# Retuned due times of a list scheduler, and five output buffers claimed ahead of the delta matmul

## Chip, cores and metric

The kernel runs on one core of one Trainium2 chip. The metric is device time in microseconds (us) of one execution. Runs are called "slow" when they lie over 1.5% above the fastest run of the same kernel. The experiments were made on three chips, with the kernel before run again beside them; its fast runs took 199.5, 199.9 and 201.6 us in the mean of each. A ratio is always to the kernel before.

## The reference, cut

Sliding-window attention, followed by a mixture of low-rank adapters over the attention output.

```python
# q, k, v: (8 batches, 8 heads, 576, 64) float32
scores = q @ k^T / 8;  masked to |i - j| <= 32
attn = softmax(scores);  x = (attn @ v) as rows of 4608 x 512
logits = x @ w_gate                       # 8 experts
w = softmax over the two largest logits   # the gate
delta = sum over the two: w * ((x @ A[e]) @ B[e])   # rank 16
return x + delta
```

## The kernel before

The program records pieces of work (`P.op`: engine, modelled duration, due time, what it depends on). A list scheduler then decides the order in which they are emitted. In the traces TensorE's pieces come in that order. So the due times change no arithmetic, only the order on each engine.

```python
# scheduler, cut: for each engine, of the pieces that can start within 0.12 us
# of the earliest one, take the one with the smallest due time
t0 = min(t for t, _ in c)
t, o = min(((t, o) for t, o in c if t <= t0 + slack),
           key=lambda x: (x[1]["due"], x[1]["i"]))
...
# PSUM buffers in the scheduler's model: strictly in turn
slots, cnt = self.pools[o["alloc"]]
prev = slots[cnt[0] % len(slots)]
```

The pieces of one batch are these (names as in the profile). Every matmul of this kernel writes a tile of the two pools in the memory PSUM; the other tiles lie in the memory SBUF.

- Loads of q, k, v on the SP queue, and casts to 16 bits on GpSimd (`c`, `vbd`).
- For each of 4 head pairs: two groups of six transposes (`tp`, then copies `qT` and `kT`), score blocks (`ps`, then `PT` by exp), and PV (`po`, then reciprocal `rc` and `xb`).
- For each batch: transposes of x (`tx`, copied to `xT`), the gating matmul `pz`, the gate on VectorE with one exp on ScalarE (result `zs`), its transposes `tz` (copied to `zT`), the delta matmuls `pd` (three pieces), output copies `obt`, and stores.

```python
ob_pool = tc.alloc_tile_pool(name="ob", bufs=3)
pw = tc.alloc_tile_pool(name="pw", bufs=3, space=PSUM)   # ps, po, pz, pd
pt = tc.alloc_tile_pool(name="pt", bufs=2, space=PSUM)   # tp, tx, tz
...
# gate on VectorE; lg lies in PSUM (pz), all other operands in SBUF
m1 = max(lg);  is1 = lg >= m1;  lm = is1 * -1e30 + lg;  m2 = max(lm);  dm = m2 - m1
dm = exp(dm)                                        # ScalarE
is2 = lm >= m2;  s = dm + 1;  s = 1 / s;  is2 = is2 * dm
gate = is1 + is2;  gate = gate * s;  zs = pz * gate
...
pd = P.op("PE", 0.43 * len(gs), d, ..., [ez, c_perm], alloc="w")
o  = P.op("ACT", ..., d, ..., [pd] + P_pd.get(len(P_pd) - 3, []))   # waits for a store
s_ = P.op("SP", 0.45 * len(gs), d + 3, ..., [o])                    # the store
```

The softmax here doesn't subtract the row's maximum and nothing guards it: scores larger than these inputs give would overflow.

## Time and profile before

| | before |
|---|---|
| device time, median of the first 3 runs | 199.71 us (199.14 to 202.63) |
| span of the profiled run | 196.4 us |
| TensorE busy | 144.3 us, 73% |
| VectorE, ScalarE, GpSimd busy | 58%, 43%, 43% |
| mean TensorE clock | 0.931 |

These lines are from the page of the kernel before. The digits are 40 slices of 4.9 us each, in tenths (9 is 90% or more). PEclk is the granted TensorE clock.

```profile
span 196.4 us, 4088 instructions
...
PE 144.3 (73%) x1600; PEld 103.8 (53%) x1600; DVE 113.8 (58%) x290; ACT 84.9 (43%) x109; POOL 84.1 (43%) x91
...
PE   0047978968389898698496898995699879958270
...
PEclk9999999999958999999669999999669999999966
DMA  5999999989999999999999589850042005102315
```

No engine is full. The DMA row is near 9 up to slice 26 (about 128 us) and then low, yet TensorE looks no busier after it than before. The clock row has three dips in the middle, at slices 12 to 13, 20 to 21 and 29 to 30, and one at the end.

The next lines are the timeline of all engines around the second dip (start, duration, engine, line, operation, output and inputs; in brackets the idle time before, and what ended it).

```profile
91.83 4.33 POOL L203 CAST vbd<-r 64x2304 f16<-64x2304 f32 x2 [3.81 <-PE po L437]
91.92 2.06 DVE L521 TENSOR_TENSOR gate<-gate,s 128x40 f32<-128x40 f32 x1
...
94.02 0.82 DVE L523 TENSOR_TENSOR zs<-pz,gate 128x640 f16<-128x640 f32 x1
...
94.89 1.01 PE L396 MATMUL ps<-mask,ident 128*128 128x512 f16 x2 [2.30 <-DVE zs L523]
...
98.52 0.61 PE L546 MATMUL pd<-B_sb,zT 128*128 128x512 f16 x1 [1.22 <-ACT zT L538]
```

A GpSimd cast starts at 91.83 us. The VectorE operation that starts just after it has 40 elements per partition and takes 2.06 us. Behind it `zs` comes late, and the score block at 94.89 us had waited 2.30 us for it, because its PSUM buffer was still held by `pz`, which `zs` reads. The delta matmul at 98.52 us waited another 1.22 us, and it starts at half clock.

The TensorE timeline of the kernel before shows another kind of wait.

```profile
79.25 0.38 PE L548 MATMUL pd<-xb,perm 128*128 128x512 f16 x1
81.22 0.92 PE L437 MATMUL po<-vbd,PT 128*128 128x130 f16 x13 [1.59 <-ACT obt L553]
```

A PV matmul waits 1.59 us for the PSUM buffer of an output copy, and that copy waits for an output buffer, which means for a store. In the waits view of the kernel before (total us, times, longest) the kinds add up as follows.

```profile
ACT obt L553 <- DMA out_dram<-obt: 6.1, 2, 3.2
...
PE ps L396 <- DVE zs L523: 4.7, 2, 2.4
...
PE po L437 <- ACT obt L553: 3.3, 2, 1.7
...
PE tp L352 <- DVE qT L358: 0.9, 1, 0.9
```

Last comes the table of stretches of the kernel before. Each stretch reaches from the last delta matmul of one batch to that of the next (columns: length, busy time of PE, PEld, DVE, ACT and POOL, granted clock, DMA share, GB/s).

```profile
60.30:79.03 18.73, 16.81 (x208) 12.61 (x206) 11.46 (x33) 8.95 (x12) 12.09 (x9) 1.00 1.11 292
79.03:102.47 23.44, 18.17 (x197) 12.99 (x196) 13.55 (x34) 11.74 (x15) 9.31 (x7) 0.85 1.06 284
102.47:123.29 20.82, 17.20 (x207) 12.64 (x205) 11.63 (x34) 10.76 (x15) 9.26 (x7) 1.00 0.87 236
123.29:145.61 22.32, 18.34 (x198) 13.11 (x196) 14.15 (x34) 10.37 (x14) 10.29 (x14) 0.85 0.32 98
145.61:164.04 18.43, 16.74 (x208) 12.61 (x206) 11.46 (x33) 10.55 (x14) 0.00 (x0) 1.00 0.14 50
```

A batch takes 18.4 to 23.4 us for 16.7 to 18.3 us of TensorE. The fourth and fifth line have little transfer left and are hardly faster (22.3 and 18.4 us; the second and first took 23.4 and 18.7 us).

### The profile page before, as it was taken

To read this page: it belongs to the slowest core of one execution; us is meant where nothing else is said; L and a number is where in the kernel's file an instruction comes from. 1 tells how busy PE (TensorE), PEld (TensorE's weight loads), DVE (VectorE), ACT (ScalarE), POOL (GpSimd) and SP (SyncE) were. 2 spreads that over 40 slices of the span, in tenths; PEclk is the share of its full clock that TensorE was granted. 3 is DMA by queue.
4 is the path that set the end of the run, shared out by engine and by line. 5 is a ranking of instruction groups with operands and counts; after the bars stand their busy time and mean duration, and the time that the engine had idled before them with its cause. 6 is when DMAs were issued, how large, how long until landed. Compare 5 with 4: busy or idle time off the path is not lost. (4 is left out here: it accounts for less than half of the span.)

```text
span 196.4 us, 4088 instructions
## 1 busy us (share of the span) xinstructions
PE 144.3 (73%) x1600; PEld 103.8 (53%) x1600; DVE 113.8 (58%) x290; ACT 84.9 (43%) x109; POOL 84.1 (43%) x91
## 2 busy tenths in 40 slices
PE   0047978968389898698496898995699879958270
PEld 0024656757237774487345674774358656845220
DVE  6876354846923873477812774759617774675500
ACT  0033354540347434653253636741465367625050
POOL 7976666748659628182507208496000000000000
PEclk9999999999958999999669999999669999999966
DMA  5999999989999999999999589850042005102315
GB/s 151 196 209 233 310 271 231 323 199 267 332 196 284 305 197 337 346 202 270 306 299 254 165 282 243 213 200 0 0 169 75 0 3 188 53 3 106 134 33 209
DMA packets 85810, 38.28 MB, mean 195 GB/s; under 512 B 44192, under 2 KB 81184, under 8 KB 85792
## 3 DMA queue, kind: packets, MB, share of 16 engines
q1 hardware_dynamic: 78464, 36.58, 68.9%
q0 software_dynamic: 4832, 0.27, 4.2%
q10 hardware_dynamic: 2496, 1.18, 2.3%
q8 instruction: 12, 0.20, 0.4%
q14 instruction: 6, 0.05, 0.1%
HBM read 28.85 MB, written 9.44 MB: 195 GB/s over the span
## 5 line engine op out<-in xcount | busy, mean ns | idle before, releaser
L352 PE MATMUL tp<-ident,c 128*128 128x128 f16 (+1 forms) x384 | 35.9, 215 | 22.0 <-POOL c L189 12.4
L408 ACT ACTIVATE PT<-ps 128x1024 f16<-128x1024 f32 x36 | 36.6, 1025 | 33.5 <-PE ps L401 33.4
L203 POOL CAST vbd<-r 64x2304 f16<-64x2304 f32 (+1 forms) x20 | 34.9, 1747 | 23.4 <-DMA out_dram<-obt 9.3
L189 POOL CAST c<-r 128x1024 f16<-128x1024 f32 (+1 forms) x36 | 31.7, 899 | 28.0 <-issue 14.4
L352 PEld LDWEIGHTS <-c 128*128 128x128 f16 (+1 forms) x384 | 25.3, 100 | 34.0 <-POOL c L189 13.1
L437 PE MATMUL po<-vbd,PT 128*128 128x130 f16 x416 | 30.1, 222 | 4.6 <-ACT obt L553 3.3
L358 DVE COPY qT<-tp 128x576 f16<-128x576 f16 x32 | 14.5, 454 | 32.0 <-PE tp L352 32.0
L437 PEld LDWEIGHTS <-PT 128*128 128x128 f16 x416 | 25.3, 98 | 7.1 <-ACT obt L553 3.9
L368 ACT COPY kT<-tp 64x576 f16<-64x576 f16 x32 | 20.3, 634 | 19.1 <-DVE kT L366 17.2
L553 ACT COPY obt<-pd 128x1024 f32<-128x1024 f32 (+1 forms) x24 | 20.4, 872 | 16.0 <-PE pd L548 8.3
L451 DVE TENSOR_TENSOR xb<-po,rc 128x640 f16<-128x640 f32 x32 | 26.4, 825 | 1.1
L396 PE MATMUL ps<-mask,ident 128*128 128x512 f16 x72 | 22.8, 400 | 4.7 <-DVE zs L523 4.7
L401 PEld LDWEIGHTS <-kT 128*128 128x128 f16 x288 | 20.3, 102 | 10.6 <-issue 1.7
L401 PE MATMUL ps<-qT,kT 128*128 128x128 f16 x288 | 24.3, 228 | 0.3 <-ACT kT L368 0.2
L546 PE MATMUL pd<-B_sb,zT 128*128 128x512 f16 x40 | 18.9, 473 | 5.6 <-ACT zT L538 5.6
L548 PE MATMUL pd<-xb,perm 128*128 128x512 f16 x40 | 18.7, 468 | 0.0
L480 DVE COPY xT<-tx 128x512 f16<-128x512 f16 x40 | 15.8, 419 | 4.1 <-PE tx L473 2.9
L366 DVE COPY kT<-tp 64x576 f16<-64x576 f16 x32 | 14.3, 446 | 5.5 <-PE tp L352 5.3
L450 DVE RECIPROCAL rc<-po 128x10 f32<-128x10 f32 x32 | 6.8, 214 | 15.1 <-PE po L437 15.1
L473 PE MATMUL tx<-ident,xb 128*128 128x128 f16 x160 | 14.2, 218 | 1.4 <-DVE xT L480 0.5
L473 PEld LDWEIGHTS <-xb 128*128 128x128 f16 x160 | 10.6, 97 | 2.6 <-issue 1.9
L513 ACT ACTIVATE dm<-dm 128x5 f32<-128x5 f32 x8 | 1.7, 208 | 22.8 <-DVE dm L511 22.8
(44 smaller groups left out, 111.1 us busy)
## 6 DMA issues: line engine op xcount, KB each, us to landing
r<-in_v_dram SPq DMA_DIRECT2D x24, 288.0 KB, 5.9
r<-in_q_dram SPq DMA_DIRECT2D x12, 512.0 KB, 5.7
r<-in_k_dram SPq DMA_DIRECT2D x12, 512.0 KB, 6.2
out_dram<-obt SPq DMA_DIRECT2D x24, 256.0 KB, 3.0
out_dram<-obt SPq DMA_DIRECT2D x16, 192.0 KB, 2.9
r<-in_q_dram SPq DMA_DIRECT2D x22, 128.0 KB, 4.0
r<-in_v_dram SPq DMA_DIRECT2D x16, 144.0 KB, 3.8
r<-in_k_dram SPq DMA_DIRECT2D x14, 128.0 KB, 4.9
```

Of the source, the lines that this page charges most:

```text
L189: eng.tensor_copy(out=qk[b, w][:, g, :, n0:n1].rearrange("p j n e d -> p e n j d"), in_=raw[b, w][:, g, :, n0:n1].rearrange("p e n (j d) - ...
L203: eng.tensor_copy(out=dst[64 * e:64 * e + 64, NB * n0:NB * n1, VD * e:VD * e + D], in_=raw[b, 2][64 * e:64 * e + 64, NB * n0:NB * n1])
L352: nc.tensor.matmul(out=o, lhsT=src[:, g, j, n] if g < 2 else sx[p0:p0 + 32, j, n], rhs=ident[p0:p0 + np_, p0:p0 + np_], is_transpose=True, ...
L368: nc.scalar.copy(out=o, in_=kt[64:128])
L396: nc.tensor.matmul(out=ps[:, i:i + 4], lhsT=ident, rhs=mask.rearrange("p r h j k -> p (r h j k)"), start=True, stop=False)
L401: nc.tensor.matmul(out=ps[:, i], lhsT=kTs[u % NQ][:, a, :], rhs=qTs[u % NQ][:, :, 32 * a:32 * a + 64].rearrange("p j (h k) -> p h j k", h= ...
L408: nc.scalar.activation(out=PTs[t % NPT][:, :, 64:192], in_=holder["t"], func=AF.Exp, scale=1.0 / float(D) ** 0.5)
L437: nc.tensor.matmul(out=po[:, GS * g:GS * g + 2 * VD], lhsT=PTs[t % NPT][:, sl, off:off + 128], rhs=vbd[b % NV][:, n, a, :], start=(i == 0) ...
L451: nc.vector.tensor_tensor(out=xs[b].rearrange("p g (e n d) -> p g e n d", e=2, n=NP)[:, :, :, n], in0=pog[:, :, :, 0:D], in1=bcast(rc, 3, ...
L473: nc.tensor.matmul(out=tp[:, 128 * c:128 * c + 128], lhsT=xs[b][:, g, 128 * c:128 * c + 128], rhs=ident, is_transpose=True, start=True, st ...
L546: nc.tensor.matmul(out=pd[:, i], lhsT=zT[:, g], rhs=B_sb, start=True, stop=False)
L553: nc.scalar.copy(out=ob[:, 0:len(gs)], in_=holder["t"][:, 0:len(gs)])
```

## The change

The change sets all due times anew, so that the scheduler's own model of the program is short. The model also gets longer transfers, five output buffers, and a claim: a delta matmul is not placed before the output buffer is free. The claim exists in the model alone; no wait is added on the hardware. Cut to its core:

```diff
+DUE = dict(ld=-10.42, cqk=-6.15, cv=-3.48, tq=-3.24, tk=-2.87, s=-0.73, e=-19.89,
+           pv=-0.4, nm=1.98, tx=-0.8, txs=0.14, pz=0.7, g0=3.1, g3=1.41, tz=2.88,
+           pd=3.21, pds=0.86, st=-7.0)
+    NOB = 5
-    ob_pool = tc.alloc_tile_pool(name="ob", bufs=3)
+    ob_pool = tc.alloc_tile_pool(name="ob", bufs=NOB)
-                xfer = P.op("DMA", (4.6 if w == 2 else 3.4) * f, d + w / 10,
+                xfer = P.op("DMA", (5.5 if w == 2 else 3.9) * f, d + w / 10,
-        e = P.op("DVE", 1.0, due_u(u, 0), lambda: norm(u, h),
+        e = P.op("DVE", 1.0, due_u(u, DUE["nm"]), lambda: norm(u, h),
-                      [ez, c_perm], alloc="w")
+                      [ez, c_perm] + P_pd.get(len(P_pd) - NOB, []), alloc="w")
-                     lambda ...: moe_ob(b, gs, h), [pd] + P_pd.get(len(P_pd) - 3, []))
+                     lambda ...: moe_ob(b, gs, h), [pd])
-            s_ = P.op("SP", 0.45 * len(gs), d + 3, ...)
+            s_ = P.op("SP", 0.45 * len(gs), d + DUE["st"], ...)
  ... (every other due time replaced in the same way)
```

This is the TensorE order around the gate of batch 2, read from the two built programs:

```
before: pz(2) | T16q T16k po14 po15 T17q T17k  ps18  tz(2) pd(2) pd(2) T18q T18k pd(2) ps19 T19q tx(3) ...
after:  pz(2) | T16q T16k ps16 T17q ps17 T17k po14 po15 T18q tz(2) ps18 T18k pd(2) tx(3) pd(2) tx(3) tx(3) ps19 ...
```

`T16q` is the transpose group of q for head pair 16. After the change more work stands between `pz` and the first piece that needs its buffer, and other work stands between `tz` and `pd` and among the `pd`.

More of the change, by code (lines that the diff above doesn't have):

```diff
@@ L301, in plan_loads @@
             f = (n1 - n0) / 4
-            d = due_u(4 * b, -7 + n0 / 4)
+            d = due_u(4 * b, DUE["ld"] + n0 / 4)
             done = {}
@@ L321, in plan_loads @@
                            + [P_pv.get(4 * (b - NV) + i) for i in range(4)])
-                    c = P.op(ce, 4.3 * f, due_u(4 * b, -2.5 + n0 / 4),
+                    c = P.op(ce, 4.3 * f, due_u(4 * b, DUE["cv"] + n0 / 4),
                              lambda n0=n0, n1=n1: cast_v(b, cn_v, n0, n1), dep)
@@ L329, in plan_loads @@
                     c = P.op(ce, (2.2 if w < 2 else 1.1) * f + (0.2 if f < 1 else 0),
-                             due_u(4 * b, -4 + n0 / 4), fn, dep)
+                             due_u(4 * b, DUE["cqk"] + n0 / 4), fn, dep)
                 for n in range(n0, n1):
@@ L373, in plan_T @@
         h = {}
-        t = P.op("PE", 0.32, due_u(u, -3), lambda: transposes(u, 0, h),
+        t = P.op("PE", 0.32, due_u(u, DUE["tq"]), lambda: transposes(u, 0, h),
                  [P_cast[b, 0, n], P_cast[b, 3, n], c_ident] + war, alloc="t")
-        e = P.op("DVE", 0.40, due_u(u, -3), lambda: evac_q(u, h), [t] + war)
+        e = P.op("DVE", 0.40, due_u(u, DUE["tq"]), lambda: evac_q(u, h), [t] + war)
         use(t, e)
         h2 = {}
-        t2 = P.op("PE", 0.32, due_u(u, -2.9), lambda: transposes(u, 1, h2),
+        t2 = P.op("PE", 0.32, due_u(u, DUE["tk"]), lambda: transposes(u, 1, h2),
                   [P_cast[b, 1, n], P_cast[b, 3, n], c_ident] + war, alloc="t")
-        e0 = P.op("DVE", 0.40, due_u(u, -2.9), lambda: evac_k(u, 0, h2), [t2] + war)
-        e1 = P.op("ACT", 0.60, due_u(u, -2.9), lambda: evac_k(u, 1, h2), [t2, e0] + war)
+        e0 = P.op("DVE", 0.40, due_u(u, DUE["tk"]), lambda: evac_k(u, 0, h2), [t2] + war)
+        e1 = P.op("ACT", 0.60, due_u(u, DUE["tk"]), lambda: evac_k(u, 1, h2), [t2, e0] + war)
         use(t2, e0, e1)
@@ L416, in plan_S @@
         h = {}
-        s = P.op("PE", 0.90, due_u(u, -1.5), lambda: score(t, h),
+        s = P.op("PE", 0.90, due_u(u, DUE["s"]), lambda: score(t, h),
                  [c_ident] + [e for x in t_units(t) for e in P_T[x]]
                  + ([P_pv[x] for x in t_units(t - NPT)] if t >= NPT else []), alloc="w")
-        e = P.op("ACT", 0.97, due_u(u, -1.5), lambda: exp(t, h),
+        e = P.op("ACT", 0.97, due_u(u, DUE["e"]), lambda: exp(t, h),
                  [s, c_PT[t % NPT]] + ([P_pv[x] for x in t_units(t - NPT)]
@@ L457, in plan_pv @@
         h = {}
-        p = P.op("PE", 0.76, due_u(u, 0), lambda: pv(u, h),
+        p = P.op("PE", 0.76, due_u(u, DUE["pv"]), lambda: pv(u, h),
                  [P_exp[t] for t in s_tiles(u)] + [P_cast[b, 2, n]] + P_x.get(b - 3, []),
                  alloc="w")
-        e = P.op("DVE", 1.0, due_u(u, 0), lambda: norm(u, h),
+        e = P.op("DVE", 1.0, due_u(u, DUE["nm"]), lambda: norm(u, h),
                  [p] + [x for x in P_x.get(b - 3, [])])
@@ L566, in plan_moe @@
             h = {}
-            t = P.op("PE", 0.23, due_u(U, 0.1 + g / 10), lambda g=g, h=h: moe_tx(b, g, h),
+            t = P.op("PE", 0.23, due_u(U, DUE["tx"] + g * DUE["txs"]), lambda g=g, h=h: moe_tx(b, g, h),
                      [P_norm[4 * b + n] for n in range(NP)], alloc="t")
-            e = P.op("DVE", 0.37, due_u(U, 0.1 + g / 10), lambda g=g, h=h: moe_xT(b, g, h),
+            e = P.op("DVE", 0.37, due_u(U, DUE["tx"] + g * DUE["txs"]), lambda g=g, h=h: moe_xT(b, g, h),
                      [t] + [P_pz.get(b - 2)])
@@ L572, in plan_moe @@
             ev.append(e)
-        pz = P.op("PE", 1.2, due_u(U, 1.0), lambda: moe_zl(b), ev + [c_w], alloc="w")
+        pz = P.op("PE", 1.2, due_u(U, DUE["pz"]), lambda: moe_zl(b), ev + [c_w], alloc="w")
         P_pz[b] = pz
-        d0 = P.op("DVE", 1.0, due_u(U, 1.1), lambda: moe_gate(b, 0), [pz])
-        d1 = P.op("ACT", 0.2, due_u(U, 1.1), lambda: moe_gate(b, 1), [d0])
-        d2 = P.op("DVE", 0.2, due_u(U, 1.15), lambda: moe_gate(b, 2), [d0])
-        d3 = P.op("DVE", 1.7, due_u(U, 1.4), lambda: moe_gate(b, 3),
+        d0 = P.op("DVE", 1.0, due_u(U, DUE["g0"]), lambda: moe_gate(b, 0), [pz])
+        d1 = P.op("ACT", 0.2, due_u(U, DUE["g0"]), lambda: moe_gate(b, 1), [d0])
+        d2 = P.op("DVE", 0.2, due_u(U, DUE["g0"] + 0.05), lambda: moe_gate(b, 2), [d0])
+        d3 = P.op("DVE", 1.7, due_u(U, DUE["g3"]), lambda: moe_gate(b, 3),
                   [d1, d2] + P_zs.get(b - 2, []))
@@ L581, in plan_moe @@
         h = {}
-        tz = P.op("PE", 0.28, due_u(U, 2.0), lambda: moe_tz(b, h), [d3], alloc="t")
+        tz = P.op("PE", 0.28, due_u(U, DUE["tz"]), lambda: moe_tz(b, h), [d3], alloc="t")
         P_zs[b] = [tz]
-        ez = P.op("ACT", 0.65, due_u(U, 2.0), lambda: moe_zT(b, h),
+        ez = P.op("ACT", 0.65, due_u(U, DUE["tz"]), lambda: moe_zT(b, h),
                   [tz] + P_zT.get(b - 2, []))
@@ L589, in plan_moe @@
             h = {}
-            d = due_u(U, 2.3 + 0.5 * i)
+            d = due_u(U, DUE["pd"] + DUE["pds"] * i)
             pd = P.op("PE", 0.43 * len(gs), d, lambda gs=gs, h=h: moe_pd(b, gs, h),
-                      [ez, c_perm], alloc="w")
+                      [ez, c_perm] + P_pd.get(len(P_pd) - NOB, []), alloc="w")
             o = P.op("ACT", 0.93 if len(gs) == 2 else 0.53, d,
-                     lambda gs=gs, h=h: moe_ob(b, gs, h), [pd] + P_pd.get(len(P_pd) - 3, []))
+                     lambda gs=gs, h=h: moe_ob(b, gs, h), [pd])
             use(pd, o)
-            s_ = P.op("SP", 0.45 * len(gs), d + 3, lambda gs=gs, h=h: moe_st(b, gs, h), [o])
-            x = P.op("DMA", 0.7 * len(gs), d + 3, lambda: None, [s_])
+            s_ = P.op("SP", 0.45 * len(gs), d + DUE["st"], lambda gs=gs, h=h: moe_st(b, gs, h), [o])
+            x = P.op("DMA", 0.7 * len(gs), d + DUE["st"], lambda: None, [s_])
             P_pd[len(P_pd)] = [x]
```

## The prediction

> **What bounds it now.** No engine is full. The page gives TensorE 144.3 us busy of 196.4 (73%), VectorE 58%, ScalarE 43%. The table of stretches shows three regimes. Up to about 58 us the loads set the pace: in the timeline the transposes of batches 1 and 2 wait 1.7 and 2.5 us for GpSimd casts. From 60 to 146 us a batch takes 20.9, 21.3, 21.5 and 22.0 us with 17.4 to 18.0 us of TensorE, although the transfers have mostly stopped by 130 us: the order of work, not the data, is the limit. From the last gating matmul, 172.4 us, 24.0 us of serial tail follow.
>
> The idle TensorE time has three sources (waits and timeline). (1) The gate: a score block waits 2.30 and 2.42 us for zs, because its PSUM buffer is held by pz. The chain is lengthened by VectorE: a 40-element multiply that normally takes 0.20 us took 2.06 us while GpSimd cast v from 91.83 us. This agrees with the Trainium skill, "SBUF — State Buffer", section "Who interferes with whom": a VectorE operation with two SBUF inputs is blocked by a GpSimd operation that reads SBUF. (2) The delta matmul waits 0.4 to 1.2 us for zT. (3) With three output buffers and stores queued behind loads (the first store is issued at 74.2 us), an output copy waits for a store, holds its PSUM buffer, and TensorE idles 1.59 and 1.69 us. Besides, the clock is 0.50 for about 6 us after each gap of kind 1, where a 512-column matmul takes 0.43 instead of 0.22 us; some 3 us are lost each time.
>
> **What changes.** No arithmetic is added or removed. In the instruction order, after the gate matmul two score blocks and four transpose groups (3.6 us from traced issue spacings) come before the first PV matmul that needs pz's buffer; zs is ready about 4.3 us after pz. A score block and a transpose group stand between tz and the delta matmul, delta matmuls alternate with the next batch's transposes, and VectorE does the normalizations after the gate. The stores of batches 0 to 3 stand before later loads, and five buffers remove wait 3. GpSimd's order hardly changes. The claim ahead of the delta matmul only steers the order; no hardware wait is added.
>
> **Cost.** Summed traced spacings give 15.4 us of TensorE per batch; with 7% of unlisted small gaps and 0.7 us of gate wait, 17.2 us (estimate). Batch 3 cannot start before its casts at 57.8 us, so nothing is won until there; loads with stores need about 16.7 us per batch (issue times), slightly under. Batch 7's transposes start at about 57.8 + 4 x 17.2 = 127 us instead of 153; the following stretch is 43 us as before, since the tail keeps its serial gate and its store. Span about 170; device time lies 2 to 3 us higher, plus an occasional slow-clock episode: **174 us**, 80% range 166 to 185. Faster by over 2%: 0.95; within 2%: 0.04; slower: 0.01.
>
> **What would show it.** Batches near 17 us between 60 and 125 us; waits for zs under 1 us each; no output copy waiting for a store; stretches at clock 0.50 fewer in the middle; the last 24 us unchanged; DMA share near 1 up to 115 us, with TensorE perhaps waiting for casts of batches 5 to 7.
>
> **What would make it wrong.** Casts colliding with the gate at new moments (up to 2 us per batch, directly exposed); loads falling behind stores, so that batch 5 to 7 transposes wait; the clock dropping more often since it follows short gaps; an order tuned to a model whose latencies differ.

## The result

The changed kernel takes 175.41 us in the median of 4 runs (173.06 to 177.03); beside it, the kernel before took 201.17 us in the median of 4. The ratio is 0.868 (95% interval 0.858 to 0.879). A ratio is the mean time of one kernel's fast runs over that of the other's of the same rounds, so it is not quite the ratio of the medians. The changed kernel's fast runs took 173.06 and 174.03 us, its slow ones 176.79 and 177.03 us.

These are the same lines of the page after the change (a slice is now 4.3 us).

```profile
span 172.3 us, 4079 instructions
...
PE 137.2 (80%) x1600; PEld 103.4 (60%) x1600; DVE 113.8 (66%) x290; ACT 85.0 (49%) x109; POOL 85.0 (49%) x91
...
PE   0028596699957999999599989997999899969180
...
PEclk9999999659995699999999999999999999999968
DMA  5999999999999899999999997976889603403425
```

TensorE is 80% busy and the clock no longer dips in the middle. A new dip stands at slices 8 and 9 (30 to 39 us), while the first batches wait for data. One is left at slices 13 and 14 (52 to 60 us), and one at the very end.

This is the table of stretches after, again from one batch's last delta matmul to the next one's.

```profile
62.33:78.42 16.09, 15.73 (x202) 12.29 (x201) 12.12 (x33) 11.06 (x15) 10.33 (x8) 1.00 1.07 272
78.42:94.98 16.56, 14.75 (x190) 11.39 (x188) 12.09 (x33) 9.94 (x14) 9.74 (x8) 1.00 1.07 268
94.98:112.07 17.09, 16.61 (x217) 13.00 (x215) 12.56 (x35) 10.87 (x15) 9.10 (x7) 1.00 0.99 283
112.07:128.35 16.28, 14.88 (x192) 11.44 (x189) 11.93 (x33) 10.18 (x14) 7.87 (x12) 1.00 0.78 220
128.35:145.77 17.42, 16.56 (x214) 13.00 (x213) 13.65 (x35) 10.75 (x15) 3.00 (x4) 1.00 0.52 157
```

A batch now takes 16.1 to 17.4 us, and TensorE is busy for 89 to 98% of it. The work of VectorE and ScalarE is the same as before (62.35 against 62.26 us and 52.80 against 52.36 us over the five stretches). TensorE's busy time fell from 87.27 to 78.54 us although it does the same matmuls: part of that is the clock, which was 0.85 in two of the stretches of before. The place of the gain can be read off the starts of these last delta matmuls: batch 0 at 60.30 us before and 62.33 after (2.0 us lost), batch 5 at 164.04 and 145.77 (20.3 us won in between), end at 196.4 and 172.3 (5.8 us won in the rest).

In the waits view after, the wait of score blocks for `zs` and the waits of PV and output copies for a store are gone. One wait has grown from 0.9 us to 8.1 us.

```profile
PE tp L360 <- DVE qT L366: 8.1, 9, 1.8
...
PE po L445 <- DVE zs L531: 0.4, 1, 0.4
```

The largest of these nine, in the timeline after:

```profile
82.94 1.04 POOL L197 CAST c<-r 128x1024 f16<-128x1024 f32 x1 [0.88 <-DMA r<-in_q_dram]
...
83.21 0.79 DVE L519 TENSOR_TENSOR dm<-m,m 128x5 f32<-128x5 f32 x1
83.92 0.44 DVE L366 COPY qT<-tp 128x576 f16<-128x576 f16 x1
...
84.41 0.38 PE L360 MATMUL tp<-ident,c 128*128 128x128 f16 x4 [1.81 <-DVE qT L366]
```

The 5-element subtraction `dm` normally takes 0.17 us. Here it takes 0.79 us beside a GpSimd cast, and `qT` stands behind it in VectorE's queue. So the cast still holds up the gate; but TensorE now loses 1.81 us once here, not 2.30 and 1.22 us and then the clock.

### The profile page after: what moved, and what is told of

Its sections match the earlier page's. It is cut to its first block, busy times and chain, and to the rows that moved or that the text cites. A ratio compares the mean times of both kernels' runs of the same rounds, so it can differ in the third digit from the quotient of the medians.

```text
span 172.3 us, 4079 instructions
## 1 busy us (share of the span) xinstructions
PE 137.2 (80%) x1600; PEld 103.4 (60%) x1600; DVE 113.8 (66%) x290; ACT 85.0 (49%) x109; POOL 85.0 (49%) x91
## 4 chain that ended last, share of the span: by engine, by line
PE 63%; DMA 13%; DVE 11%; ACT 4%; SPq 2%; issue 2%; ACTq 2%; POOL 1%
PE po L445 13%; PE tp L360 10%; DMA r<-in_k_dram 10%; PE ps L404 8%; PE ps L409 7%; PE pz L497 6%; PE pd L554 6%; PE tx L481 5%; PE pd L556 5%; DMA r<-in_q_dram 3%; DVE dm L519 2%; SPq L175 2%; ACT PT L416 2%; PE tz L541 2%; DVE qT L366 2%
## 5 line engine op out<-in xcount | busy, mean ns | idle before, releaser
L360 PE MATMUL tp<-ident,c 128*128 128x128 f16 (+1 forms) x384 | 37.0, 219 | 23.8 <-POOL c L197 11.6
L360 PEld LDWEIGHTS <-c 128*128 128x128 f16 (+1 forms) x384 | 26.3, 101 | 34.5 <-POOL c L197 12.8
L197 POOL CAST c<-r 128x1024 f16<-128x1024 f32 (+1 forms) x36 | 32.3, 906 | 28.2 <-DMA r<-in_k_dram 15.3
L376 ACT COPY kT<-tp 64x576 f16<-64x576 f16 x32 | 20.3, 634 | 32.1 <-DVE kT L374 31.7
L445 PE MATMUL po<-vbd,PT 128*128 128x130 f16 x416 | 28.7, 220 | 1.1 <-ACT PT L416 0.7
L409 PEld LDWEIGHTS <-kT 128*128 128x128 f16 x288 | 21.7, 107 | 10.6 <-issue 3.6
L404 PE MATMUL ps<-mask,ident 128*128 128x512 f16 x72 | 24.5, 426 | 0.0
L554 PE MATMUL pd<-B_sb,zT 128*128 128x512 f16 x40 | 16.0, 400 | 1.6 <-ACT zT L546 1.6
L556 PE MATMUL pd<-xb,perm 128*128 128x512 f16 x40 | 15.9, 399 | 0.0
L481 PE MATMUL tx<-ident,xb 128*128 128x128 f16 x160 | 13.3, 221 | 0.0
L497 PE MATMUL pz<-WA_sb,xT 128*128 128x136 f16 x160 | 10.8, 223 | 0.0
```

The source lines that it names most:

```text
L197: eng.tensor_copy(out=qk[b, w][:, g, :, n0:n1].rearrange("p j n e d -> p e n j d"), in_=raw[b, w][:, g, :, n0:n1].rearrange("p e n (j d) - ...
L360: nc.tensor.matmul(out=o, lhsT=src[:, g, j, n] if g < 2 else sx[p0:p0 + 32, j, n], rhs=ident[p0:p0 + np_, p0:p0 + np_], is_transpose=True, ...
L404: nc.tensor.matmul(out=ps[:, i:i + 4], lhsT=ident, rhs=mask.rearrange("p r h j k -> p (r h j k)"), start=True, stop=False)
L409: nc.tensor.matmul(out=ps[:, i], lhsT=kTs[u % NQ][:, a, :], rhs=qTs[u % NQ][:, :, 32 * a:32 * a + 64].rearrange("p j (h k) -> p h j k", h= ...
L445: nc.tensor.matmul(out=po[:, GS * g:GS * g + 2 * VD], lhsT=PTs[t % NPT][:, sl, off:off + 128], rhs=vbd[b % NV][:, n, a, :], start=(i == 0) ...
L481: nc.tensor.matmul(out=tp[:, 128 * c:128 * c + 128], lhsT=xs[b][:, g, 128 * c:128 * c + 128], rhs=ident, is_transpose=True, start=True, st ...
```

## The experiments

**The two halves of the change.** With all compute due times and the rest set back, the scheduler gives exactly the order of before, so the change can be cut in two without remainder. `p_compute` has the new due times of TensorE, VectorE and ScalarE pieces only; `p_mem` has the rest. The scheduler decides anew for each half, so their orders are close to, not equal to, the halves of the changed kernel's order.

```diff
# p_compute, against the changed kernel
-DUE = dict(ld=-10.42, cqk=-6.15, cv=-3.48, ..., st=-7.0)
+DUE = dict(ld=-7, cqk=-4, cv=-2.5, ..., st=3.0)
-    NOB = 5                        # and the old claim, the old transfer times
+    NOB = 3
# p_mem, against the changed kernel
-DUE = dict(..., tq=-3.24, tk=-2.87, s=-0.73, e=-19.89, pv=-0.4, nm=1.98, ...)
+DUE = dict(..., tq=-3, tk=-2.9, s=-1.5, e=-1.5, pv=0, nm=0, ...)   # all old
```

> New due times for the compute pieces only; loads, casts and stores keep their old due times, three output buffers and the old claim. Theory A (the order of the TensorE, VectorE and ScalarE pieces is the gain): most of the 26 us, 176 to 183 us, ratio 0.88 to 0.91 to the kernel before. Rival B (the output buffers and the earlier stores are the gain): 193 us or more.

> The other half: new due times of loads, casts and stores, the new claim and five output buffers, with the old compute due times. The TensorE order is that of the kernel before but for one place. Theory A: only the two waits of 1.59 and 1.69 us for a store, and what follows from them, go: 193 to 198 us. Rival B: 180 us or less.

`p_compute` took 184.6 us in the mean of three fast runs (the slow one 188.63), ratio 0.925 (0.913 to 0.937), just above the expected range. `p_mem` took 189.28 and 189.55 us in its fast runs and 196.0 and 198.07 us in its slow ones. The fast pair over the 199.5 us of the kernel before's fast runs is 0.949; with two runs I give it no interval. So I had put too much on the compute order and too little on the other half. The product of the two, 0.925 x 0.949 = 0.878, is near the measured 0.868: the halves roughly multiply. Rival B, that the buffers and stores are the gain, falls; but they have a share in it.

**Three buffers in the new order.** The pool alone was changed; the order is exactly that of the changed kernel.

```diff
-    ob_pool = tc.alloc_tile_pool(name="ob", bufs=NOB)
+    ob_pool = tc.alloc_tile_pool(name="ob", bufs=3)
```

> The changed kernel in exactly its order, with three output buffers instead of five. Theory A: stores stand before loads, so most land in time; only batch 4, whose output copy comes at 125 us while the store of batch 3 is issued at 125.5 us, waits about 4 us: 176 to 181 us. Rival B: 190 us or more.

It took 178.0 us in the mean (177.21 to 178.73), ratio 0.892 (0.884 to 0.900) against 0.868 for five buffers. They were run at other times. The size was as expected, about 4 us (against 173.5 us); the place was not. Output copies wait for stores eight times, 12.5 us in all, spread over the batches, and TensorE loses about 1 us in each of five waits on them.

**Five buffers in the old order.** This is the same single edit on the kernel before.

```diff
-    ob_pool = tc.alloc_tile_pool(name="ob", bufs=3)
+    ob_pool = tc.alloc_tile_pool(name="ob", bufs=5)
```

> The kernel before in exactly its order, five output buffers instead of three, nothing else. Theory E: the two TensorE waits of 1.6 us for an output copy go, the gate collisions stay: 194 to 198 us. If the store order in the run with the old compute order and the new stores (189.4 us in its fast runs) was what counted, this is 197 us or more; if the buffers were, 188 to 192 us.

It took 197.3 us in the mean of three fast runs, ratio 0.987 (0.970 to 1.004). The two waits of TensorE for an output copy are gone, as expected, but the gain is at most some 3%, and the interval reaches no gain. Of the two readings for the 0.949 of `p_mem`, buffers alone (188 to 192 us) falls; most of that gain came with the new times of loads and stores.

**The gate's collisions, in the old order.** The Trainium skill, "SBUF — State Buffer", section "Who interferes with whom", says that a VectorE instruction with two SBUF inputs contends with a GpSimd instruction that reads SBUF, and that one with at most one SBUF input, outside the two-port modes, does not. So a few of the gate's small operands were moved into the unused columns of `pz` in PSUM. Nothing else changed.

```diff
+            for i, name in enumerate(("m2", "dm")):
+                st[b, name] = pzg[:, :, ER + 3 * E + i]
+            for i, name in enumerate(("i2d", "g12")):
+                st[b, name] = pzg[:, :, ER + E + E * i:ER + 2 * E + E * i]
-  is2 = is2 * dm;  gate = is1 + is2;  gate = gate * s
+  i2d = is2 * dm;  g12 = is1 + i2d;   gate = g12 * s     # i2d, g12, m2, dm in PSUM
```

> The kernel before in its order; the gate's small operands are placed so that no VectorE operation of the gate has two SBUF inputs (some lie in the free columns of pz in PSUM). Theory C (GpSimd casts hold up the gate on VectorE: 6.7 us in all, in three of eight gates, each followed by a slow-clock episode): the long gate operations of 0.8 to 2.1 us go back to 0.2 us, the waits of score blocks for zs fall from 2.3 and 2.4 us to under 1 us and one or two slow-clock episodes go: 188 to 194 us. Rival D (the order alone makes the wait): 198 us or more.

The collisions went as theory C says. The source view of the last gate multiply (duration in ns: shortest, median, longest) in the kernel before reads:

```profile
L521 DVE TENSOR_TENSOR gate<-gate,s x8: 199/201/2059, 52.5 to 184.7; 128x40 f32<-128x40 f32 x8
```

and in this run:

```profile
L526 DVE TENSOR_TENSOR gate<-pz,s x8: 199/199/199, 48.1 to 184.7; 128x40 f32<-128x40 f32 x8
```

No gate operation of this run exceeds 205 ns (`zs` aside, which takes 0.82 us in every run), and the waits of score blocks for `zs` fell from 2.3 and 2.4 us to at most 0.52 us each. Yet the time was 197.6 us in the mean of fast runs, ratio 0.990 (0.977 to 1.003): theory C's time was missed. The slow clock did not go either, it moved: its mean is 0.919 in this profile against 0.931 before. The TensorE timeline shows where the gain went.

```profile
72.66 0.38 PE L553 MATMUL pd<-xb,perm 128*128 128x512 f16 x1
83.65 1.59 PE L437 MATMUL po<-vbd,PT 128*128 128x130 f16 x13 [10.61 <-ACT obt L558]
```

And this is ScalarE in the same stretch:

```profile
82.59 1.93 ACT L558 COPY obt<-pd 128x1024 f32<-128x1024 f32 x2 [11.95 <-DMA out_dram<-obt]
```

The last delta matmul of batch 1 started at 72.7 us instead of 79.3 us. But the store whose output buffer the next copy needs stood behind loads in the SP queue and was issued at 75.9 us. ScalarE waited 11.95 us, a PV matmul 10.61 us, and the clock fell again after it. The time won was handed back to the next limit, one batch later.

**Both limits lifted.** The next run has the same operands in PSUM and five output buffers, in the old order.

> The kernel before in its order, gate operands in PSUM as in the run before_psumgate, and five output buffers instead of three. In before_psumgate the time won at the gates was lost again in one wait of 10.6 us of a PV matmul for an output copy, which waited for a store. Theory E (the late stores cap the kernel before, and hid the gate's cost): with five buffers that wait shrinks to under 4 us and the time won stays: 186 to 192 us. Rival (the gate's collisions cost little): 195 us or more.

It took 191.4 us in the mean (190.01 to 192.56, all fast), ratio 0.960 (0.942 to 0.978). Five buffers without the PSUM operands took 197.3 us. So the collisions cost the old order about 5.9 us (191.4/197.3 = 0.970), and this shows only once the stores no longer cap it. Theory E's time is met, at its upper end, but the wait did not shrink to under 4 us: ScalarE waits 6.3 us for a store, and a PV matmul 5.0 us for the exp behind it.

**The same operands in PSUM in the new order.** The edit is that of `before_psumgate`, on the changed kernel.

> The changed kernel in its order, with the gate's operands in PSUM so that GpSimd casts don't hold up VectorE. Gate operations over 0.25 us vanish (they cost some 6 us of VectorE in the changed kernel, five of eight gates). Theory C: in the new order about half of it was exposed: 169 to 172 us. Rival H (the new order hides it): 173 us or more.

Fast runs took 172.00 and 172.87 us (ratio 0.863, 0.835 to 0.890), slow ones 175.72 and 176.38 us, against 173.06 and 174.03 us of the changed kernel. It was run at another time. About 1 us is within what I can't resolve. It is at the edge between the two theories' ranges and settles neither. The gate operations over 0.25 us are gone, as expected. Its batches 0 to 4 are 4.6 to 5.4 us ahead of the changed kernel's (last delta matmul of batch 0 at 57.76 us, of batch 4 at 123.38), but batch 5 is only 2.6 us ahead, and ScalarE waits 13.3 us in all for stores, where the changed kernel shows no such wait. Again a gain runs into the output buffers.

**The compute order by itself.** The next kernel is `p_mem` with the gate operands in PSUM. It has the old compute order, but neither collisions at the gate nor three buffers hold it up. It differs from `after_psumgate` in the compute due times alone.

```diff
# p_mem, with the PSUM operands of before_psumgate
```

> Old compute order, with new due times of loads, casts and stores, five output buffers, and gate operands in PSUM: neither collisions with GpSimd nor output buffers hold this order up. Against the run after_psumgate (172.4 us in its fast runs) it differs in the compute order alone. Theory A (the order has a gain of its own): 181 to 187 us. Rival I (the order's gain was only that it dodged collisions and late stores): 172 to 177 us.

Its one fast run took 181.97 us, its three slow ones 184.73 to 186.87 us. `after_psumgate` took 172.4 us in the mean of its fast runs. That is 9.5 us of difference, as theory A expected, or about 8 us if the ratios are compared (181.97/201.6 = 0.903 and 0.863), with the caution that one fast run is little. They were run at other times. Rival I falls: the new compute order is worth something by itself, not only because it dodges collisions and late stores. But the run shows more. With the old compute order, 201.6 us came down to 181.97 us, so a large part of what was lost in the kernel before can be had without touching the compute order. And against `before_psumgate_5buf` (0.960), which also has five buffers and no collisions, it differs in the due times of loads, casts and stores, the model's transfer times and the claim: together these are worth some 6%, where the prediction had counted two waits of 1.6 and 1.7 us.

**Without the loads.** Batches 2 to 7 use the raw data of batches 0 and 1 again. Their outputs are wrong, which doesn't matter for the times.

```diff
     def raw_tile(b, w):
+        if b >= 2:
+            for x in ((0, 3) if w == 0 else (w,)):
+                raw[b, x] = raw[b - 2, x]
+            return
     def load_qk(...), load_v(...):
+        if b >= 2:
+            return
```

> The kernel before in its order, but batches 2 to 7 use again the loaded data of batches 0 and 1 (wrong result on purpose): no load after batch 1, so no wait for data, and stores are not held up behind loads. If the prediction's reading holds (order, not data, sets the pace from 60 us on), 186 to 194 us. If loads and late stores set the pace, 180 us or less.

> The changed kernel in its order with the same removal of loads after batch 1 (wrong result on purpose). If the changed kernel is still bound by TensorE and its order, only the waits for data up to 58 us go, and it saves 3 to 8 us: 166 to 171 us. If it has become bound by its transfers, it falls below 163 us.

The kernel before without loads took 197.9 us in its fast runs, ratio 0.981 (0.971 to 0.992). The changed one took 174.1 us (172.43 to 174.79), ratio 0.863 (0.856 to 0.871), against 0.868 with all its loads. Both are above the expected ranges: the loads are worth even less than I thought. But the removal also moves the casts. In the profile of the kernel before without loads (a slow run) they lengthen the gate of batch 0 more than before, and its last delta matmul starts at 63.95 us instead of 60.30 us. From there to the last delta matmul of batch 5 it takes 99.7 us against 103.7 us with loads. So from 60 us on, loads and what they hold up are worth about 4 us of 104 in this profile (perhaps somewhat more in a fast run), and the order sets the pace; that the changed kernel had become bound by transfers is excluded. The saving of 3 to 8 us that I expected from the early waits for data did not come. The timeline of the changed kernel without loads shows why.

```profile
46.00 3.99 POOL L205 CAST c<-r 128x1024 f16<-128x1024 f32 x4
...
47.99 1.04 DVE L533 TENSOR_SCALAR s<-dm 128x5 f32<-128x5 f32 x1
...
50.92 4.33 POOL L219 CAST vbd<-r 64x2304 f16<-64x2304 f32 x2
51.06 2.02 DVE L537 TENSOR_TENSOR gate<-gate,s 128x40 f32<-128x40 f32 x1
...
54.35 0.75 PE L368 MATMUL tp<-ident,c 128*128 128x128 f16 x6 [4.34 <-DVE qT L374]
```

With the data there, the casts run one behind the other (46.0 to 55.3 us) and fall on the gate of batch 0. Its operations take 1.04 and 2.02 us where 0.16 and 0.20 us are normal, and a transpose waits 4.34 us behind them. The last delta matmul of batch 0 starts at 62.35 us, against 62.33 us with all loads; from there to that of batch 5 it takes 80.9 us against 83.4 us.

**Buffers in turn.** The scheduler's model hands out PSUM buffers strictly in turn. The built program does not: in the changed kernel 8 of 112 transpose tiles get the bank of the tile just before, so that the second of two transpose groups waits until the first is copied out. By theory F this is the wait for `qT`. In this run each tile has a buffer of its own and they go in turn; the order is unchanged.

```diff
-    pw = tc.alloc_tile_pool(name="pw", bufs=3, ...)      # tag "w"
-    pt = tc.alloc_tile_pool(name="pt", bufs=2, ...)      # tag "t"
+    pw = tc.alloc_tile_pool(name="pw", bufs=1, ...)      # tags w0, w1, w2 in turn
+    pt = tc.alloc_tile_pool(name="pt", bufs=1, ...)      # tags t0, t1 in turn
```

> The changed kernel in its order, but each PSUM buffer is taken strictly in turn, as the scheduler's model assumes; in the changed kernel the pool hands out the same bank twice in a row for 8 of 112 transpose tiles, and 23 of 97 wide tiles don't take the bank of the third one before. Theory F (the model and the pool disagree, and that is the wait of TensorE transposes for the qT copy, 8.1 us in nine waits): these waits fall below 3 us, 169 to 173 us against 173.5 in the fast runs of the changed kernel. Rival G (the waits come from the queue of VectorE anyway): no change, within 1 us.

The waits view of this run (its profile is from a slow run):

```profile
PE po L450 <- DVE zs L536: 7.0, 6, 2.0
...
PE tp L365 <- DVE qT L371: 2.3, 1, 2.3
```

The wait for `qT` fell from 8.1 us to 2.3 us, so theory F names a cause of it. It is not the only one, for rival G has a share: in `after_psumgate`, with the pool's choice but without collisions on VectorE, the wait was 4.2 us, and with both changes, in the run `after_best` below, 0.5 us. Both theories missed the time: it rose to 177.0 us in the mean of fast runs (ratio 0.886, 0.865 to 0.907), and PV now waits for `zs` six times, 7.0 us in all. With the pool's free choice PV gets a buffer that is already free; strictly in turn it gets the one that `pz` still holds. For the wide tiles the deviation from the model helped: in `after_best`, where they go as the pool likes again, no PV waits for `zs`.

**A version with three additions.** It has the operands in PSUM; the two transpose banks in turn, the wide tiles as the pool likes; and 45 idle transposes after the last `pz`, to keep the clock up for the last delta matmuls.

```diff
+        if b == B - 1:
+            P.op("PE", 2.5, due_u(U, DUE["pz"]), fill, [pz], alloc="t")
+    def fill():
+        tp = pt.tile([128, 1024], F16, tag=ttag(), name="fill")
+        for i in range(45):
+            nc.tensor.matmul(out=tp[:, 0:128], lhsT=ident, rhs=ident,
+                             is_transpose=True, start=True, stop=True)
```

> The changed kernel with three additions: gate operands in PSUM; the two transpose banks strictly in turn (the wide PSUM tiles as the pool likes, since the run after_rot brought waits for zs there); and 45 idle transposes, 2.5 us, after the last gating matmul, to keep the TensorE clock up for the last delta matmuls. Against the changed kernel's 173.5 us in fast runs: 0 to 1 us from PSUM operands, 1 to 3 us from the transpose banks, 1.3 us from the clock at the end: 168 to 171.5 us.

The result is correct. It took 171.92 us in the median and 169.88 and 171.29 us in its fast runs. The ratio to the kernel before is 0.846 (0.837 to 0.855), against 0.868 (0.858 to 0.879) of the changed kernel. They were run at other times. The fast runs are in the expected range. The intervals do not overlap, so I count it as about 2% faster. What each addition brought was not measured apart. The profile, from a slow run, shows the end of the TensorE timeline:

```profile
158.82 2.12 PE L583 MATMUL fill<-ident 128*128 128x128 f16 x35
161.94 0.45 PE L551 MATMUL tz<-perm,zs 128*128 128x128 f16 x5 [1.00 <-DVE zs L541]
163.17 0.39 PE L564 MATMUL pd<-B_sb,zT 128*128 128x512 f16 x1 [0.79 <-ACT zT L556]
```

The idle transposes fill the gap in which the changed kernel waits 3.26 us before `tz`; `tz` does not come sooner for them (4.9 us after the start of `pz`, against 4.6 us). But the delta matmuls behind it run at full clock (1.00 from 159 to 165 us), where the changed kernel's fall to half clock. And it shows the next limit, on ScalarE:

```profile
95.22 0.59 ACT L571 COPY obt<-pd 128x512 f32<-128x512 f32 x1 [5.62 <-DMA out_dram<-obt]
```

An output copy waits 5.62 us for a store, and the `kT` copies of the next transposes stand behind it in ScalarE's queue. More output buffers, or stores placed earlier still, would be the next thing to try. That was not run.

## Why the prediction was right

The measured median is 175.4 us for 174 predicted, the fast runs at 173.5. Point by point:

- **The order, not the data, sets the pace from 60 us on.** Leaving out the loads gave ratios of 0.981 and 0.863 for the kernel before and the changed one, and about 4 of 104 us and 2.5 of 83 us between batches 0 and 5. The order that counts is not that of the compute pieces alone: that of loads and stores has a share (see `p_mem_psumgate`).
- **17.2 us of each batch.** Measured 16.1 to 17.4 us in the table of stretches, and 16.6 us between the transposes of batches 3 and 7 ((131.42 - 64.89)/4). The estimate came from traced issue spacings plus an allowance for gaps; it was 0.6 us too long.
- **Batch 3 starts at 57.8 us.** This step was mis-sized. Its casts did end at 57.8 us, as predicted, but TensorE reached its transposes at 64.89 us. The prediction took the earliest possible start for the start. Before it lay the collisions at the gate of batch 0 and a stretch of slow clock that the new order had not removed. These are the last cast that the transposes of batch 3 need, their start, and two lines of the table of 5 us stretches (the clock is the third number from the end):

```profile
56.77 1.04 POOL L204 CAST c<-r 64x1024 f16<-64x1024 f32 x1 [0.84 <-PE tz L541]
...
64.89 0.53 PE L360 MATMUL tp<-ident,c 128*128 128x128 f16 x6
...
50.00:55.00 5.00, 3.47 (x28) 2.41 (x28) 4.83 (x14) 1.98 (x4) 3.28 (x5) 0.72 1.19 305
55.00:60.00 5.00, 4.43 (x33) 3.18 (x34) 1.78 (x4) 2.87 (x4) 3.35 (x3) 0.60 0.97 191
```

- **43 us from the transposes of batch 7 to the end.** Measured 40.9 us (172.3 - 131.4). The three errors, +7.1, -2.3 and -2.1 us, sum to 2.7 us on a predicted span of about 170 us. So the total is better than its terms, and part of the hit is luck.
- **Waits for `zs` under 1 us, no output copy waiting for a store, no slow clock in the middle.** All as predicted: 0.43 us, none, and 1.00 in every stretch from 62 to 146 us. (The last `tz`, in the tail, waits 3.26 us for `zs` before and after; the prediction left the tail as it was.)
- **Three sources of idle time.** They are real, but the prediction wrote them side by side as if each could be had by itself. The runs showed that they stand in series: with the gate's collisions gone, a wait of 10.6 us for a store took the gain back (ratio 0.990), and five buffers alone gave 0.987; together they gave 0.960 (0.942 to 0.978).
- **Five buffers and earlier stores.** The prediction gave them the 1.6 and 1.7 us waits alone. In the new order the buffers are worth about 4 us (0.892 against 0.868), and the half of the change with buffers, claim and early stores measured 0.949, though five buffers alone gave 0.987 in the old order.
- **What was not foreseen.** The new wait for `qT`, because the pool does not hand out buffers as the model does and because casts hold up VectorE's queue; and that GpSimd collisions stay as long as before, hidden at one place and paid at another.
- **A slip of wording.** The "last gating matmul" at 172.4 us was the one before the last (its end); the last one starts at 181.25 us. From the one that was meant, the tail was 24.0 us before and is 23.0 us after (172.3 - 149.3).

Two things stay open. The due times were tried in two groups only, so which of them matter most is not known. Nor was the claim ahead of the delta matmul tried by itself; it always came with the new times of loads and stores.

## What to carry to other kernels

When an in-order kernel is limited by its order, read the gain from the stretch between two equal events of successive batches, and cost the new order by summing traced issue spacings; but take the start from what stands before it on the engine, not from the arrival of its data. Waits found in one profile can stand in series, as here: lift one alone, and look in the profile for the wait that took its time before calling it cheap. A scheduler that works on a model of buffers should be checked against the buffers that the built program really uses; here the difference cost about 6 us of waits at one place (8.1 to 2.3 us) and saved 7 us at another.

## What the Trainium skill lacked or had wrong

- "SBUF — State Buffer", section "Who interferes with whom", was right here: VectorE operations with two SBUF inputs rose from 0.20 to 2.06 us beside a cast, a `tensor_scalar` from 0.16 to 1.04 us, while the reciprocal and the small operations with one PSUM input stayed at 0.19 to 0.20 us in all eight gates. What it does not spell out is the remedy and its worth: with one input moved to PSUM, no gate operation exceeded 0.205 us, and the kernel with five buffers won 3%.
- "TensorE: Matmul & The Clock Gate", section "HAM oscillation — how this bites in real kernels", gives as the rule that TensorE should have no idle gap over about 3.4 us. Here one gap of 2.30 us (ending at 94.89 us) was followed by a clock of 0.50 from 95 to 100 us, and one of 2.42 us (ending at 137.90 us) by one of 0.50 from 139 to 145 us, while after a gap of 1.81 us (ending at 84.41 us in the changed kernel) the clock stayed at 1.00. So gaps shorter than the rule's can cost the clock here. The length of the gap does not decide it alone: after one of 2.49 us (ending at 44.96 us in the kernel before) the clock stayed at 1.00 up to 53 us.
- No page says in which order a tile pool hands out its buffers. Here two transpose tiles in a row got the same bank in 8 of 112 cases.
